# Masking attention weights by comparing exponentials with one constant instead of scores with a threshold per tile

## The chip, the cores and the metric

The kernel runs on one core of one Trainium2 chip. The metric is the device time of one execution in microseconds (us), lower is better. The engines of the core are named as in the profile: PE is the matrix engine (PEld its weight loads), DVE the vector engine, ACT the scalar engine, POOL the GpSimd engine, SP the engine that issues the DMAs. SBUF is the on-chip working memory; PSUM is the small memory that PE writes, in banks.

## What is computed

There are 8 batches of 8 heads, 576 positions, head size 64, then a feed-forward layer on 4608 tokens (512 to 2048 to 512). All inputs and outputs are float32.

```python
scores = scale * np.matmul(q, k.transpose(0, 1, 3, 2))
thresh = np.max(scores, axis=-1, keepdims=True) - tau        # tau = 0.02
scores = np.where(scores >= thresh, scores, -1000000000.0)
scores = scores - np.max(scores, axis=-1, keepdims=True)
attn = np.exp(scores)
attn = attn / (np.sum(attn, axis=-1, keepdims=True) + 1e-09)
attn_out = np.matmul(attn, v)
...
h = x @ w_in                       # x: attn_out, heads side by side
g = np.maximum(h, 0.0) + np.log1p(np.exp(-np.abs(h)))
out = g @ w_out
```

A score survives if it lies within tau of its row's maximum; the others get weight zero.

## The kernel before

The attention is cut into 32 units, a unit being two heads of one batch, and a unit into 9 tiles of 128 query rows by 576 keys, 288 tiles in all. In a unit a row of a tile holds one head's query, tile 4 the rests of both heads. The feed-forward work is cut into chunks of tokens and is dealt out between the attention tiles, a quota of matmuls for each tile, so that PE has work while a tile goes through the other engines.

A tile goes through these steps, and the names are those of the functions:

- `scores` (L490): PE makes the 128 by 576 scores, in two halves of 288 columns, in one of two PSUM buffers `s` (`SB` = 2). The weights and queries are split in high and low parts, so four matmuls (eight in tile 4) make one tile.
- `row_max`: DVE reduces the scores to minus the row's maximum, `negm`.
- `exps`: ACT writes exp(score + negm) into one of the three slots of `e_all` in SBUF (`EB` = 3), and with a second, tiny instruction the threshold `thr` = max - tau.
- `mask`: DVE compares the scores, still in PSUM, with `thr`, multiplies the exponentials by the result, in place, and sums the row.
- For the first five units (`whole`), PE turns the masked tile over by transposes and works in float32. For the others, `weights_hi` has POOL write the float16 high part `h` (scaled by 2 to the 15th) and `weights_lo` has DVE write the low part from `e_all` and `h`; a DMA transposes both (`eT<-h` in the profile), and `values` multiplies them with v (tile `vt`, product `pv`).

Ahead of these, k and q are split (`k`, `q` on POOL, from `kn`, `qn`) and turned over (`tr` on PE, `kT`, `qT` on ACT). In the feed-forward, `hidden` makes `h<-xh,w_i` and `h<-xl,w_i` on PE; ACT applies the softplus into `st`; POOL splits that in two float16 parts `g`; `project` makes `o<-w_o,g`, and ACT or DVE adds it into `acc`. POOL also splits the attention's result (`xp`, then `xh` and `xl`). In the first third of the time the feed-forward's weights are prepared as well: DVE reassembles them from words (`wa_i`, `wa_o` from `wc_i`, `wc_o`), and ACT and POOL split them (`w_i`, `w_o`).

The order of the work is set in two ways. The letters of a string, `PAT`, say which step comes when within a tile: while tile g is dealt with, `R` takes the maximum of tile g+2, `e` its exponentials, `m` masks tile g+1, `h` makes the high part of g+1, `l` the low part of g, `f` is feed-forward work, `S` the scores of tile g+3. So tile g+3's scores take the PSUM buffer that tile g+1 had. From tile 36 on (`TQ`), the instructions of DVE, ACT and POOL keep the order in which they are written, by the class `Queue`; its one line, L156, is the line that the profile shows for nearly all instructions of these three engines. Those of PE and of SP, and all of them before tile 36, are put in order by the compiler's scheduler, which lets an instruction go ahead of others when it thinks its data and buffers free.

Of the kernel before, what the change touches and what calls it, by code (L numbers as in the profile page):

```python
# [9 lines left out]
F32 = mybir.dt.float32  # L10
# [3 lines left out]
AF = mybir.ActivationFunctionType  # L14
ALU = mybir.AluOpType
AX = mybir.AxisListType
# [8 lines left out]
P = 128  # L25
# [40 lines left out]
def tile_kernel(ctx: ExitStack, tc: tile.TileContext, q, k, v, tau, w_in, w_out, out):  # L66
# [8 lines left out]
    nc = tc.nc  # L75
# [5 lines left out]
    HS = S // 2  # L81
# [7 lines left out]
    cpool = ctx.enter_context(tc.tile_pool(name="cpool", bufs=1))  # L89
    wpool = ctx.enter_context(tc.tile_pool(name="wpool", bufs=3))  # L90
    apool = ctx.enter_context(tc.tile_pool(name="apool", bufs=2))
# [17 lines left out]
    ntau = cpool.tile([P, 1], F32, name="ntau")  # L109
    nc.vector.tensor_scalar(out=ntau, in0=tau_sb, scalar1=-1.0, scalar2=None, op0=ALU.mult)  # L110
    nc.vector.tensor_tensor(out=ntau, in0=ntau, in1=tau_sb, op=ALU.min)
    qscale = cpool.tile([P, 1], F32, name="qscale")
    nc.vector.tensor_scalar(out=qscale, in0=tau_sb, scalar1=0.0, scalar2=SCALE,
                            op0=ALU.is_ge, op1=ALU.mult)
# [48 lines left out]
    vec = Queue(nc.vector)  # L163
    act = Queue(nc.scalar)
# [172 lines left out]
    for b in range(B):  # L337
        for hp in range(NPAIR):
            s = Unit()
# [151 lines left out]
                                 start=(m == 0), stop=(m == len(parts) - 1))  # L491

    def row_max(s, t):
        negm = apool.tile([P, 1], F32, tag="negm", bufs=3, name=f"negm_{s.i}_{t}")
        thr = apool.tile([P, 1], F32, tag="thr", bufs=3, name=f"thr_{s.i}_{t}")
        vec.reduce_max(negm, s.sp[t][:, :, 0:HS], axis=AX.XY, negate=True)
        s.m[t] = (negm, thr)

    def exps(s, t):
        act.activation(s.e[t].rearrange("p (h n) -> p h n", h=2), s.sp[t][:, :, 0:HS],  # L500
                             AF.Exp, bias=s.m[t][0], scale=1.0)
        act.activation(s.m[t][1], s.m[t][0], AF.Identity, bias=ntau, scale=-1.0)

    def mask(s, t):
        e2 = s.e[t].rearrange("p (h n) -> p h n", h=2)
        masked.append(vec.scalar_tensor_tensor(
            out=e2, in0=s.sp.pop(t)[:, :, 0:HS], scalar=s.m.pop(t)[1], in1=e2, op0=ALU.is_ge, op1=ALU.mult,
            accum_out=s.sums[:, t:t + 1]))

# [419 lines left out]
    for kind, g in WL:  # L931
        for m in range(4):
            n = len(prep)
# [74 lines left out]
    u0.eng, u0.eng_lo = eng, pool  # L1008
    scores(*tiles[0])
    row_max(*tiles[0])  # L1010
    exps(*tiles[0])
    scores(*tiles[1])
    row_max(*tiles[1])
    exps(*tiles[1])
    mask(*tiles[0])
    scores(*tiles[2])
    load_v(units[1])

    done = 0.0
    for g, (cur, t) in enumerate(tiles):  # L1020
# [7 lines left out]
        for step in PAT:  # L1028
# [6 lines left out]
            elif step == "h" and nxt and not nxt[0].whole:  # L1035
                weights_hi(*nxt)
            elif step == "l" and not cur.whole:
                weights_lo(cur, t)
            elif step == "R" and ahead:
                row_max(*ahead)  # L1040
            elif step == "e" and ahead:
                exps(*ahead)
            elif step == "m" and nxt:
                mask(*nxt)
            elif step == "f":
                upto += quota / PAT.count("f")
                while done < upto:
                    done += next(ffn)
            elif step == "x":
                extras(cur.i, t)  # L1050
            elif step == "S" and g + 3 < NS:
                scores(*tiles[g + 3])
            elif step == "v":
                slow_products()
            elif step == "w":
                while prep and prep[0][0] <= g:
                    _, f, a = prep.pop(0)
                    f(*a)
            elif step == "p":
                point()  # L1060
# [40 lines left out]
```

## Time and profile before

| | |
|---|---|
| median of 3 runs | 1302.42 us (1301.31 to 1306.54) |
| the profiled execution | 1300.2 us, of it the span of instructions 1298.4 us |
| PE busy | 1231.9 us, 95% of the span |
| DVE, ACT, POOL busy | 931.2, 906.2, 912.7 us |

The span has four stretches: about 20 us of start; up to about 400 us attention together with the preparation of the weights (the whole units up to 167 us); up to 1147 us attention together with feed-forward chunks; and then feed-forward work alone. Busy times are sums over the span; what an engine's time is worth in one stretch is read from the views of that stretch. "Idle before" in a group, and the list of waits, say which instruction ended an engine's idle time. A matmul's shown time overlaps with the next one's, so a busy PE can still hold short gaps.

### The profile page before, as it was taken

The numbers are of one execution on the slowest core, as the hardware profiler recorded it, in microseconds if no ns is written. First come the engines' busy times: TensorE is split into PE (matmuls) and PEld (weight loads), VectorE is DVE, ScalarE is ACT, GpSimd is POOL, SyncE is SP. The second block draws the span as 40 slices with busy tenths as digits, with TensorE's granted clock in tenths as the row PEclk, the third lists the DMA queues.
The fourth block names the chain that finished last, engine by engine and source line by source line (L and its number), as shares of the span: only waits on it lengthen the run. The fifth ranks groups of instructions, "written<-read, shape, count | busy, mean of one in ns | idle before, by whom it ended". The sixth has DMA issues, their size and how long they took to land.

```text
span 1298.4 us, 21573 instructions
## 1 busy us (share of the span) xinstructions
PE 1231.9 (95%) x7045; PEld 741.9 (57%) x7045; DVE 931.2 (72%) x1738; ACT 906.2 (70%) x1715; POOL 912.7 (70%) x986
## 2 busy tenths in 40 slices
PE   6988987898999999999999999999999999999998
PEld 5655544454566566556555655665657755554455
DVE  6878888989878887788778977786677666640111
ACT  5877887877777777777777787778676767744321
POOL 2577788978876787778776886688667777564332
PEclk9999999999999999999999999999999999999999
DMA  4544458865877788778777787787667665520010
GB/s 130 161 140 125 129 131 166 174 123 122 174 146 147 144 168 163 151 144 175 144 148 144 168 148 148 145 153 147 129 128 162 115 132 106 101 66 17 1 42 17
DMA packets 368737, 167.90 MB, mean 129 GB/s; under 512 B 320208, under 2 KB 346224, under 8 KB 368624
## 3 DMA queue, kind: packets, MB, share of 16 engines
q1 hardware_dynamic: 368624, 166.52, 61.6%
q8 instruction: 56, 0.92, 0.3%
q14 instruction: 57, 0.47, 0.1%
HBM read 56.62 MB, written 10.63 MB: 52 GB/s over the span
## 4 chain that ended last, share of the span: by engine, by line
PE 42%; ACT 17%; DVE 15%; POOL 13%; issue 8%; DMA 4%; SPq 0%; POOLq 0%; DVEq 0%; ACTq 0%
PE o L789 14%; PE h L725 14%; PE s L490 7%; ACT st L156 5%; ACT L156 5%; POOL g L156 4%; DVE e_all L156 3%; DVE h L156 3%; PE pv L605 3%; DVE negm L156 3%; ACT e_all L156 2%; PE pv L559 2%; POOL xl L156 2%; DMA eT<-h 2%; POOL h L156 2%
## 5 line engine op out<-in xcount | busy, mean ns | idle before, releaser
L789 PE MATMUL o<-w_o,g 128*128 128x512 f16 x1728 | 407.1, 381 | 3.3 <-DVE xp L156 1.5
L725 PE MATMUL h<-xh,w_i 128*128 128x512 f16 (+1 forms) x1280 | 361.3, 359 | 4.5 <-ACT kT L156 2.0
L156 POOL TENSOR_SCALAR h<-e_all 128x576 f16<-128x576 f32 x243 | 228.5, 943 | 112.6 <-DVE e_all L156 110.3
L156 ACT ACTIVATE e_all<-s,negm 128x576 f32<-128x576 f32 x288 | 213.6, 742 | 116.6 <-DVE negm L156 110.5
L725 PEld LDWEIGHTS <-w_i 128*128 128x128 f16 x1920 | 179.9, 98 | 168.8 <-issue 11.7
L156 DVE SCALAR_TENSOR_TENSOR e_all<-s,thr,e_all 128x576 f32<-128x576 f32 x288 | 232.8, 809 | 48.9 <-ACT thr L156 48.8
L156 DVE TENSOR_REDUCE negm<-s 128x1 f32<-128x576 f32 x288 | 214.9, 746 | 66.5 <-PE s L490 64.8
L789 PEld LDWEIGHTS <-g 128*128 128x128 f16 x1728 | 159.7, 98 | 176.4 <-issue 7.0
L156 DVE SCALAR_TENSOR_TENSOR h<-e_all,h 128x576 f16<-128x576 f32 x243 | 236.4, 973 | 20.2 <-POOL h L156 19.6
L725 PE MATMUL h<-xl,w_i 128*128 128x512 f16 (+1 forms) x640 | 230.2, 360 | 1.4 <-POOL xl L156 1.3
L156 POOL TENSOR_SCALAR g<-st 128x512 f16<-128x512 f32 x144 | 97.8, 679 | 164.6 <-ACT st L156 162.4
L156 DVE SCALAR_TENSOR_TENSOR acc<-o,c,acc 128x512 f32<-128x512 f32 x108 | 80.1, 743 | 154.5 <-PE o L789 154.1
L156 POOL TENSOR_TENSOR g<-st,g 128x512 f16<-128x512 f32 x144 | 171.9, 1194 | 12.0
L490 PE MATMUL s<-kT,q 128*128 128x288 f32 x768 | 152.7, 328 | 19.3 <-DVE e_all L156 16.7
L156 ACT ACT_TABLE_LOAD x119 | 152.7, 1283 | 4.1 <-DVE negm L156 1.9
L490 PEld LDWEIGHTS s<-kT,q 128*128 128x128 f32 x768 | 114.7, 192 | 57.1 <-DVE e_all L156 44.7
L605 PE MATMUL pv<-eT,vt 128*128 128x288 f16 x972 | 140.6, 288 | 3.9 <-DVE xp L156 2.4
L156 ACT ACTIVATE st<-h,c 128x512 f32<-128x512 f32 x144 | 91.0, 683 | 76.3 <-PE h L725 75.5
L490 PE MATMUL s<-kT,qT 128*128 128x288 f32 x512 | 106.2, 329 | 10.1 <-DVE e_all L156 9.8
L605 PEld LDWEIGHTS <-vt 128*128 128x128 f16 x972 | 89.3, 98 | 38.1 <-issue 5.3
L156 ACT COPY xp<-pv 64x288 f32<-64x288 f32 (+3 forms) x133 | 50.5, 384 | 78.3 <-PE pv L605 74.1
L156 ACT ACTIVATE st<-st,c 128x512 f32<-128x512 f32 x144 | 96.2, 715 | 2.3
(112 smaller groups left out, 1513.8 us busy)
## 6 DMA issues: line engine op xcount, KB each, us to landing
q<-q SPq DMA_DIRECT2D x62, 192.0 KB
kn<-in_k_dram SPq DMA_DIRECT2D x32, 256.0 KB
qn<-in_q_dram SPq DMA_DIRECT2D x32, 256.0 KB
vn<-in_v_dram SPq DMA_DIRECT2D x32, 256.0 KB
wc_i<-in_moe_w_in_dram SPq DMA_DIRECT2D x16, 512.0 KB
wc_o<-in_moe_w_out_dram SPq DMA_DIRECT2D x16, 512.0 KB
qT<-qT SPq DMA_DIRECT2D x62, 128.0 KB
out_dram<-acc SPq DMA_DIRECT2D x14, 512.0 KB
```

The source lines that it names most:

```text
L156: i = getattr(self.eng, name)(*args, **kwargs)
L490: nc.tensor.matmul(sp[:, hf, 0:HS], lhs, s.kT[j][:, hf * HS:(hf + 1) * HS], start=(m == 0), stop=(m == len(parts) - 1))
L559: nc.tensor.matmul(o[0:D, 0:n], s.vn[k_, v_slot(j, c), :], h[k_, c, 0:n], start=(c == 0), stop=(c == NC))
L605: nc.tensor.matmul(o[:, 0:HS], s.vt[:, a, :], s.eT[j][:, b, x0:x0 + HS], start=(n == 0), stop=(n == 2 * NC))
L725: nc.tensor.matmul(bank[:, i * u.T:(i + 1) * u.T], wi[g, cc][:, a, e], x[cc], start=(cc == 0 and m == 0), stop=(cc == NCC - 1 and m == 2))
L789: nc.tensor.matmul(o, u.g[fc][m // 2][:, sl], wo[fc][:, m % 2, :], start=(n == 0), stop=(n == 3 * QF - 1))
```

## The change

Once, at the start, ACT makes `cut` = exp(-tau) (`ntau`, an existing column, is -tau). The mask compares a tile's exponentials with `cut`, as exp(s - max) >= exp(-tau) says the same as s >= max - tau. The threshold `thr` of each tile is no longer made. The mask's two tensor inputs are then both the tile's slot of `e_all` in SBUF; before, one was `e_all` and the other the scores in PSUM. The scores are last read by the exponentials.

```diff
+    cut = cpool.tile([P, 1], F32, name="cut")
+    nc.scalar.activation(cut, ntau, AF.Exp)
...
     def row_max(s, t):
-        negm = apool.tile([P, 1], F32, tag="negm", bufs=3, name=f"negm_{s.i}_{t}")
-        thr = apool.tile([P, 1], F32, tag="thr", bufs=3, name=f"thr_{s.i}_{t}")
-        vec.reduce_max(negm, s.sp[t][:, :, 0:HS], axis=AX.XY, negate=True)
-        s.m[t] = (negm, thr)
+        s.m[t] = apool.tile([P, 1], F32, tag="negm", bufs=3, name=f"negm_{s.i}_{t}")
+        vec.reduce_max(s.m[t], s.sp[t][:, :, 0:HS], axis=AX.XY, negate=True)

     def exps(s, t):
-        act.activation(s.e[t].rearrange("p (h n) -> p h n", h=2), s.sp[t][:, :, 0:HS],
-                             AF.Exp, bias=s.m[t][0], scale=1.0)
-        act.activation(s.m[t][1], s.m[t][0], AF.Identity, bias=ntau, scale=-1.0)
+        act.activation(s.e[t].rearrange("p (h n) -> p h n", h=2), s.sp.pop(t)[:, :, 0:HS],
+                       AF.Exp, bias=s.m.pop(t), scale=1.0)

     def mask(s, t):
-        e2 = s.e[t].rearrange("p (h n) -> p h n", h=2)
         masked.append(vec.scalar_tensor_tensor(
-            out=e2, in0=s.sp.pop(t)[:, :, 0:HS], scalar=s.m.pop(t)[1], in1=e2, op0=ALU.is_ge, op1=ALU.mult,
-            accum_out=s.sums[:, t:t + 1]))
+            out=s.e[t], in0=s.e[t], scalar=cut, in1=s.e[t], op0=ALU.is_ge, op1=ALU.mult, accum_out=s.sums[:, t:t + 1]))
```

On DVE the order of a tile's steps stays. Before, around tiles 2 to 4 of a unit in the third stretch (`s` are the score buffers, `h` the float16 weights, numbers at the ends of names only tell tiles apart):

```order
L156 TENSOR_REDUCE negm_3_6721<-s_131 128x1
L156 SCALAR_TENSOR_TENSOR e_all,sums_6576<-s_130,thr_2_6687,e_all 128x576
L156 SCALAR_TENSOR_TENSOR h_132<-e_all,h_132 128x576
L156 TENSOR_REDUCE negm_4_6757<-s_130 128x1
L156 SCALAR_TENSOR_TENSOR e_all,sums_6576<-s_131,thr_3_6722,e_all 128x576
L156 SCALAR_TENSOR_TENSOR h_132<-e_all,h_132 128x576
```

and with the change, at the same place on DVE (L158 is the same line, two lines further down):

```order
L158 TENSOR_REDUCE negm_3_6429<-s_133 128x1
L158 SCALAR_TENSOR_TENSOR e_all,sums_6290<-e_all,cut 128x576
L158 SCALAR_TENSOR_TENSOR h_134<-e_all,h_134 128x576
L158 TENSOR_REDUCE negm_4_6463<-s_132 128x1
L158 SCALAR_TENSOR_TENSOR e_all,sums_6290<-e_all,cut 128x576
L158 SCALAR_TENSOR_TENSOR h_134<-e_all,h_134 128x576
```

Nothing moved there: the maximum, the mask and the low part follow each other as before, and only what the mask reads is another.

On ACT at that place stands before (`st` is the softplus of a feed-forward block):

```order
L156 ACTIVATE e_all<-s_130,negm_2_6686 128x576
L156 ACTIVATE thr_2_6687<-negm_2_6686,ntau 128x1
L156 ACTIVATE e_all<-s_131,negm_3_6721 128x576
L156 ACTIVATE thr_3_6722<-negm_3_6721,ntau 128x1
L156 ACTIVATE rt_6754<-rT_6746 9x128
L156 ACTIVATE e_all<-s_130,negm_4_6757 128x576
L156 ACTIVATE thr_4_6758<-negm_4_6757,ntau 128x1
L156 ACT_TABLE_LOAD
L156 ACTIVATE st_15_6788<-h_15_6734,c_2_5147 128x512
```

and now:

```order
L158 ACTIVATE e_all<-s_132,negm_2_6396 128x576
L158 ACTIVATE e_all<-s_133,negm_3_6429 128x576
L158 ACTIVATE rt_6460<-rT_6452 9x128
L158 ACTIVATE e_all<-s_132,negm_4_6463 128x576
L158 ACT_TABLE_LOAD
L158 ACTIVATE st_15_6492<-h_15_6440,c_2_4923 128x512
```

One instruction a tile is gone, and the rest keeps its order.

On PE the scheduler puts some tiles' scores earlier among the other matmuls, as it thinks their buffer free sooner. This is most marked in the second stretch. Before, the scores of tile 1 of unit 7 stand inside the output block `o_1_2`, whose first products are already behind them:

```order
L789 LDWEIGHTS g_0_5_2362
L789 MATMUL o_1_2_2904<-w_o_1_2104,g_0_5_2362 128x512
L490 MATMUL s_130<-kT_0_2657,q_95 128x288 x4
L789 LDWEIGHTS g_0_5_2363
L789 MATMUL o_1_2_2904<-w_o_1_2104,g_0_5_2363 128x512
L789 LDWEIGHTS g_0_6_2697
```

and now the same scores stand ahead of that block:

```order
L787 LDWEIGHTS g_0_7_2616
L787 MATMUL o_1_1_2725<-w_o_3_2109,g_0_7_2616 128x512
L432 MATMUL tr_1_1_2741<-identr,q_7_1_2649 128x128 x4
L492 MATMUL s_132<-kT_0_2541,q_97 128x288 x4
L787 LDWEIGHTS g_0_4_2236
L787 MATMUL o_1_2_2778<-w_o_0_1961,g_0_4_2236 128x512
```

So these scores moved ahead of some products of the feed-forward and of the values; elsewhere in the third stretch most scores stand where they stood.

## The prediction

> **What bounds the kernel now.** I read the totals first, then the busy times by stretch, then the waits of PE, and last the single instructions around a mask.
>
> ```profile
> span 1298.4 us, 21573 instructions
> PE 1231.9 (95%) x7045; PEld 741.9 (57%) x7045; DVE 931.2 (72%) x1738; ACT 906.2 (70%) x1715; POOL 912.7 (70%) x986
> ...
> 20.00:400.00 380.00, 342.89 (x1886) 207.78 (x1885) 323.54 (x609) 304.66 (x641) 291.38 (x301) 0.98 0.61 140
> 400.00:1147.00 747.00, 736.10 (x4351) 451.75 (x4349) 575.48 (x1070) 547.49 (x984) 557.33 (x604) 1.00 0.73 143
> ...
> 240.00:280.00 40.00, 33.09 (x183) 19.68 (x182) 39.49 (x70) 29.79 (x60) 31.16 (x29) 0.96 0.69 144
> 320.00:360.00 40.00, 39.08 (x230) 24.13 (x231) 34.34 (x61) 29.50 (x53) 33.38 (x36) 1.00 0.81 173
> ```
>
> A row by stretch gives its length, then the busy us of PE, PEld, DVE, ACT and POOL, the granted clock, and the share and rate of the DMAs. From 400 to 1147 us PE is busy 736 of 747 us: PE sets the time, and the other engines have a quarter to spare (DVE 171.5 us idle, POOL 189.7). From 20 to 400 us PE has 37 us of gaps, and DVE is the tightest of the others with 56.5 us idle. The last two rows show how far DVE may be loaded: at 34.3 of 40 us PE still runs at 39.1; at 39.5 of 40 PE is down to 33.1. What is left outside these stretches, start and end, has two masks or none.
>
> ```profile
> PE s L490 <- DVE e_all L156: 26.5, 31, 3.3
> PE s L490 <- DVE e_all L156: 18.5, 18, 1.9
> PE s L490 <- DVE e_all L156: 4.8, 12, 0.6
> ```
>
> These are the waits of PE's scores for the mask to give the PSUM buffer back: over the whole span, from 20 to 400 us, and from 400 to 1147 us (us in total, times, longest).
>
> **The change part by part.**
>
> *The buffer comes free sooner.* It is now given back by the exponentials, and these run a step of the tile pipeline ahead of the mask. That takes away at most the 26.5 us above. But scores that come early are worth PE time only where the rest keeps up, and some scores now stand earlier on PE, ahead of products that could have run meanwhile. I take half of the first part (-9 us of 18.5, at 20 to 400 us) and most of the second (-4 us of 4.8); ends 0 and -26.5.
>
> *The threshold goes from ACT, and DVE's wait for it.*
>
> ```profile
> L156 ACT ACTIVATE thr<-negm,ntau 128x1 f32<-128x1 f32 x288 | 83.2, 289 | 0.1
> L156 DVE SCALAR_TENSOR_TENSOR e_all<-s,thr,e_all 128x576 f32<-128x576 f32 x97 | 78.4, 809 | 14.6 <-ACT thr L156 14.6
> L156 DVE SCALAR_TENSOR_TENSOR e_all<-s,thr,e_all 128x576 f32<-128x576 f32 x189 | 152.8, 809 | 34.2 <-ACT thr L156 34.2
> ```
>
> ACT loses 83.2 us of 906. ACT bounds no stretch (304.66 of 380, 547.49 of 747), so by itself this is worth nothing. The two mask rows are those of 20 to 400 and 400 to 1147 us (97 and 189 masks): DVE waited 48 times for `thr`; the exponentials come 0.29 us earlier than `thr` did, so 48 x 0.29 = 14 us of DVE's idle time goes, which is idle time and not work. I count it as cover for what follows, not as a gain.
>
> *The mask reads SBUF twice.* This is the term that decides.
>
> ```profile
> L156 DVE SCALAR_TENSOR_TENSOR e_all<-s,thr,e_all x288: 798/808/819, 17.4 to 1144.3; 128x576 f32<-128x576 f32 x144
> L156 POOL TENSOR_SCALAR h<-e_all x243: 661/1112/1717, 167.2 to 1145.2; 128x576 f16<-128x576 f32 x122
> L156 DVE SCALAR_TENSOR_TENSOR h<-e_all,h x243: 744/916/1999, 171.0 to 1146.8; 128x576 f16<-128x576 f32 x122
> L156 DVE TENSOR_TENSOR xp<-pv,xp x108: 439/456/463, 216.0 to 1158.8; 64x288 f32<-64x288 f32 x108
> L156 DVE SCALAR_TENSOR_TENSOR wa_o<-wc_o,wa_o x32: 673/1096/1815, 81.3 to 278.9; 128x512 uint32<-128x512 uint32 x32
> ...
> 605.78 0.75 DVE L156 SCALAR_TENSOR_TENSOR h<-e_all,h 128x576 f16<-128x576 f32 x1
> 605.95 1.11 POOL L156 TENSOR_SCALAR h<-e_all 128x576 f16<-128x576 f32 x1 [1.07 <-DVE e_all L156]
> 607.49 0.80 DVE L156 SCALAR_TENSOR_TENSOR e_all<-s,thr,e_all 128x576 f32<-128x576 f32 x1
> 607.78 1.41 POOL L156 TENSOR_TENSOR k<-kn,k 128x576 fp32r<-128x576 f32 x1
> 608.22 1.58 DVE L156 SCALAR_TENSOR_TENSOR h<-e_all,h 128x576 f16<-128x576 f32 x1
> ```
>
> The first five rows give the shortest, the middle and the longest duration in ns. Instructions of DVE with one input in PSUM (the mask, `xp<-pv,xp`) always take the same time. Those with both inputs in SBUF (`h<-e_all,h`, `wa_o<-wc_o,wa_o`) take up to 2.7 times their shortest. The five rows of the timeline (start, duration) show why: POOL's `k` ran from 607.78 to 609.19; DVE's low part, begun at 608.22, ended at 609.80, 0.61 us after POOL's end. The other way round, DVE's low part ended at 606.53, and POOL's `h`, begun at 605.95, at 607.06, 0.53 us after it. Such a pair doesn't overlap in its main part. The mask at 607.49, with one SBUF input, ran its 0.80 us while POOL's `k` began and took no longer. With the change the mask belongs to the other kind.
>
> In "SBUF — State Buffer", section "Who interferes with whom", the Trainium skill states the same split: a DVE instruction with two SBUF inputs contends with a GpSimd instruction that reads SBUF, one with at most one such input does not. This speaks against the change, and the rows here bear it out.
>
> Alone, the new mask should take the 744 ns of the low part of the same 576 columns, 0.065 us under today's 809. Its wait for POOL isn't in the trace. From below: the low part's own mean wait, 973 - 744 = 229 ns, from the row at the end of this part. From above: POOL is in an instruction for 291.38 / 380 = 0.77 of 20 to 400 us, a mean one lasts 291.38 / 301 = 0.97 us, and if each mask had to wait for a whole one that is 0.74 us. I take half a POOL instruction, as a mask can come at any point of it: 0.77 x 0.48 = 0.37 us; and 557.33 / 747 x 0.46 = 0.34 us for 400 to 1147 us. Net of the 0.065 us, that is 97 x 0.305 = 30 us more DVE time in the second stretch and 189 x 0.275 = 52 us in the third. No cover is left if DVE's idle time ends.
>
> Behind the mask on DVE stands the low part. A POOL instruction that the mask held up goes first when the mask ends, and then holds up the low part: I take 0.1 us for each of the 243 (5 us and 19 us by stretch), between 0 and 0.4. POOL in turn is held up by masks, at most 0.61 us each; of its 88.6 us idle at 20 to 400 us and 189.7 us later the masks take 97 x 0.77 x 0.61 = 46 us and 189 x 0.75 x 0.61 = 86 us at most. POOL stays under its stretch's length.
>
> What is late next, then, is DVE. At 20 to 400 us it gets 35 us more work, 323.5 + 35 = 358.5 of 380, between the two 40 us rows above. Half of the 35, 17.5 us, I let through to the end, as some of DVE's idle time is true waiting for ACT, POOL and PE. From 400 to 1147 us it becomes 575.5 + 71 = 646 of 747 = 0.87, as loaded as at 320 to 360 us, where PE kept 0.98: I let 8% through, 6 us.
>
> ```profile
> L156 DVE SCALAR_TENSOR_TENSOR h<-e_all,h 128x576 f16<-128x576 f32 x243 | 236.4, 973 | 20.2 <-POOL h L156 19.6
> ...
> 3.66 0.16 DVE L111 TENSOR_TENSOR ntau<-ntau,tau_sb 128x1 f32<-128x1 f32 x1
> 5.04 0.67 ACT L156 CAST k<-kn 128x576 fp32r<-128x576 f32 x1 [3.02 <-DMA kn<-in_k_dram]
> ```
>
> *The constant.* It is ACT's first instruction, ready when `ntau` is, at 3.82 us, and short as `thr`, 0.29 us: done at 4.1, while ACT waits for `kn` until 5.04. It costs nothing, and if `kn` came a microsecond earlier, a few tenths.
>
> **The sum.** -9 - 4 + 17.5 + 6 = +10.5 us on the profiled execution's 1300.2 us. The median of the runs, 1302.4, lies 2.2 us above that execution, so the forecast is 1300.2 + 10.5 + 2.2, about 1313 us.
>
> **The rivals.**
>
> *The early buffer wins (the other side).* If the mask's two inputs, which are one and the same tile, go by one read, it doesn't hold POOL up; no row shows an instruction that reads one tile twice. Or POOL and DVE have the slack to take the waits. Then the 26.5 us of waits for the buffer go, less a fifth for scores that now wait for the exponentials: -21 us, 1281 us. It decides where the mask's mean wait stays under some 0.1 us, or where less than a fifth of DVE's added work comes through. For it speaks that the scores' start hung on the mask in 31 waits of PE; against it, the split of the rows above, without an exception.
>
> *Hidden anyway.* DVE's idle time of 56.5 and 171.5 us takes the new waits, and the saving at the buffer is as large as what comes through: 1302 us. For it speaks the row of 320 to 360 us; against it 240 to 280 us, where DVE has half a microsecond left.
>
> *The port is the bound.* The same section of the Trainium skill says that the lock is exclusive and is held for the full instruction. As a mechanism of this kernel: if a pair of such instructions could not overlap at all, POOL's 848.7 us from 20 to 1147, less the 243 x (943 - 661 ns) = 68 us that its `h` already waits, and DVE's 243 x 0.744 + 64 x 0.673 (`wa_i` taken as `wa_o`) + 288 x 0.744 us would have to fit one after another: 781 + 438 = 1219 us in 1127, 92 us too much.
>
> ```profile
> L156 POOL TENSOR_SCALAR h<-e_all 128x576 f16<-128x576 f32 x243 | 228.5, 943 | 112.6 <-DVE e_all L156 110.3
> ```
>
> The trace bears it out in part: what follows the release is 0.61 of 0.744 us and 0.53 of 0.661 us, so each instruction overlaps by 0.13 us, and over 905 of POOL's and 595 of DVE's that gives 195 us back. It then fits, at 0.91 of the time. As other POOL rows also hold waits, 92 us is an upper end; I set this rival at +60 us, 1362.
>
> **How the numbers follow.** Some of the new waits come through (1306 to 1345, likeliest 1313): 0.43. Hidden (1296 to 1309): 0.24, of which a fifth lies on either side. The early buffer wins (1272 to 1296): 0.25. The port as the bound (1345 to 1380): 0.08. A change of under 0.5%, 6.5 us, can't be told from none here. So faster 0.27, same 0.26, slower 0.47. The slower case's own range is 1306 to 1345; the range that leaves 2 in 10 out reaches from 1279, into the early buffer's case, to 1346.
>
> **What would show it.** The mask's shortest time near 744 ns, its middle near 1.0 us and its longest near 2 us would show the contention; 740 to 760 throughout would show the one read. POOL's `k`, `g` and `q`, whose shortest times are whole today, should lengthen on average. No `thr` on ACT, and the scores' waits named after ACT's `e_all` and much shorter. DVE near 358 of 380 us in the second stretch if the sum holds. I am wrong if PE's gaps from 20 to 400 us shrink below 30 us (the early buffer wins), or if PE from 400 to 1147 us falls under 0.96 (the port).

## The result, and the profile after

The kernel with the change takes 1356.2 us (median of 4 runs, 1355.58 to 1356.88), the kernel before 1301.87 us in the runs beside it: 1.041 times as long, with an interval of 1.038 to 1.044. The direction of the forecast was right; its size was not: +54 us against +10.5, and outside the range.

The totals of the profile after:

```profile
span 1353.8 us, 21257 instructions
PE 1241.1 (92%) x7045; PEld 756.4 (56%) x7045; DVE 1033.2 (76%) x1738; ACT 855.0 (63%) x1428; POOL 999.8 (74%) x986
...
PEclk9988889889999999999999999999999999999999
```

DVE's busy time grew by 102.0 us and POOL's by 87.1, with the same number of instructions on each; ACT lost 51 us. Neither DVE nor POOL is near the span.

The two stretches of attention (length, then PE, DVE, ACT and POOL as in the prediction's rows; the third stretch ends with the last mask, which now lies near 1200 us):

```profile
20.00:400.00 380.00, 325.62 (x1742) 200.36 (x1742) 339.55 (x578) 269.26 (x515) 301.02 (x281) 0.93 0.56 131
400.00:1200.00 800.00, 758.82 (x4475) 471.35 (x4474) 657.68 (x1095) 532.13 (x824) 632.44 (x623) 0.99 0.70 137
```

From 20 to 400 us PE did 1742 matmuls instead of 1886, and at the rate of before 144 of them are 29 us. From 400 to 1200 us it did 4475, which at the rate of before (4351 in 747 us) would have taken 768 us: 32 us. The counts are rough (together 61 us, where the span grew by 55), but by them the loss comes about half from each stretch, though only a third of the masks lie in the first. The two lose in different ways. Up to 400 us, PE's idle time grew from 37 to 54 us, and the mean matmul got longer (325.62 / 1742 = 0.187 us of busy time, 0.182 before); the granted clock fell from 0.98 to 0.93. After 400 us nearly all of the loss is idle time, which grew from 11 to 41 us.

The mask, the low part and POOL's `h` (shortest, middle and longest in ns), then the groups with the mean and what ended the idle time before them:

```profile
L158 DVE SCALAR_TENSOR_TENSOR e_all<-e_all,cut x288: 799/825/2019, 18.1 to 1201.7; 128x576 f32<-128x576 f32 x144
L158 DVE SCALAR_TENSOR_TENSOR h<-e_all,h x243: 743/995/1972, 184.4 to 1203.8; 128x576 f16<-128x576 f32 x122
L158 POOL TENSOR_SCALAR h<-e_all x243: 660/1112/1197, 180.6 to 1202.6; 128x576 f16<-128x576 f32 x122
...
L158 DVE SCALAR_TENSOR_TENSOR e_all<-e_all,cut 128x576 f32<-128x576 f32 x288 | 295.7, 1027 | 26.4 <-ACT e_all L158 26.2
L158 DVE SCALAR_TENSOR_TENSOR h<-e_all,h 128x576 f16<-128x576 f32 x243 | 273.6, 1126 | 42.2 <-POOL h L158 42.2
L158 POOL TENSOR_TENSOR vt<-vn,vt 128x640 f16<-128x640 f32 x27 | 48.2, 1786 | 2.3
```

and POOL's `vt` before:

```profile
L156 POOL TENSOR_TENSOR vt<-vn,vt 128x640 f16<-128x640 f32 x27 | 39.4, 1459 | 2.3
```

The mask, which never left 798 to 819 ns before, now takes up to 2019: it contends. Its mean grew from 809 to 1027 ns (288 x 0.218 = 63 us), the low part's from 973 to 1126 (243 x 0.153 = 37 us). POOL's `vt` took 1459 ns before and takes 1786.

Five of PE's waits after (us, times, longest; `s` is the one for the score buffer, `topv` a small tile made from v), and the instruction of PE that gained most idle time ahead of it, after (L425) and before (L423):

```profile
PE tr L425 <- DVE xp L158: 32.6, 16, 2.5
...
PE tr L425 <- DVE topv L158: 6.0, 1, 6.0
...
PE pv L603 <- DVE xp L158: 4.9, 5, 1.1
...
PE s L492 <- ACT e_all L158: 4.1, 3, 2.2
...
PE o L787 <- DVE xp L158: 3.7, 3, 1.8
...
L425 PE MATMUL tr<-identr,k 128*128 128x128 f32 x64 | 20.2, 316 | 43.5 <-DVE xp L158 32.6 <-DVE topv L158 6.0 <-ACT gw L158 2.6
```

```profile
L423 PE MATMUL tr<-identr,k 128*128 128x128 f32 x64 | 20.4, 318 | 2.0 <-DVE acc L156 0.7 <-DVE xp L156 0.5 <-ACT gw L156 0.2
```

The wait for the score buffer went from 26.5 to 4.1 us, as the early release promised. In its place PE now idles 43.5 us, 2.0 before, ahead of the transposes of k, mostly until DVE's `xp<-pv,xp` gives a PSUM buffer back. Of the 32.6 us of that wait only 3.6 lie before 400 us, so it is a matter of the time after that. How it comes about is seen at the end of a unit, in the timeline of after (start, duration):

```profile
600.83 1.21 DVE L158 SCALAR_TENSOR_TENSOR h<-e_all,h 128x576 f16<-128x576 f32 x1 [1.68 <-POOL h L158]
...
602.63 0.80 DVE L158 SCALAR_TENSOR_TENSOR e_all<-e_all,cut 128x576 f32<-128x576 f32 x1
602.71 1.98 POOL L158 TENSOR_TENSOR vt<-vn,vt 128x640 f16<-128x640 f32 x1
...
603.36 1.93 DVE L158 SCALAR_TENSOR_TENSOR h<-e_all,h 128x576 f16<-128x576 f32 x1
...
605.22 0.44 DVE L158 TENSOR_TENSOR xp<-pv,xp 64x288 f32<-64x288 f32 x1
...
605.72 0.28 PE L425 MATMUL tr<-identr,k 128*128 128x128 f32 x1 [2.53 <-DVE xp L158]
```

The mask, begun at 602.63, holds up POOL's `vt`; that then has its turn and holds up DVE's low part until 605.29, 1.93 us instead of the 0.74 that it takes alone. `xp` stands behind the low part on DVE, and PE's transpose behind `xp`. So 1.93 less 0.74, about 1.2 us, of the 2.53 us for which PE idles here go back to this collision, with a mask that itself waited for nothing. DVE was late already, as the low part before had waited 1.68 us for POOL's `h`.

### The profile page after: what moved, and what is told of

Its sections match the earlier page's. It is cut to its first block, busy times and chain, and to the rows that moved or that the text cites. A ratio compares the mean times of both kernels' runs of the same rounds, so it can differ in the third digit from the quotient of the medians.

```text
span 1353.8 us, 21257 instructions
## 1 busy us (share of the span) xinstructions
PE 1241.1 (92%) x7045; PEld 756.4 (56%) x7045; DVE 1033.2 (76%) x1738; ACT 855.0 (63%) x1428; POOL 999.8 (74%) x986
## 4 chain that ended last, share of the span: by engine, by line
PE 29%; POOL 22%; DVE 22%; issue 12%; ACT 9%; DMA 4%; SPq 1%; POOLq 0%; ACTq 0%; DVEq 0%
PE o L787 11%; PE h L723 10%; POOL g L158 7%; DVE e_all L158 5%; DVE h L158 5%; DVE negm L158 5%; POOL h L158 4%; PE s L492 3%; ACT st L158 3%; ACT L158 2%; PE pv L603 2%; POOL xl L158 2%; DVE wa_o L158 2%; POOL q L158 2%; ACT e_all L158 2%
## 5 line engine op out<-in xcount | busy, mean ns | idle before, releaser
L787 PE MATMUL o<-w_o,g 128*128 128x512 f16 x1728 | 412.9, 387 | 5.5 <-DVE xp L158 3.7
L723 PE MATMUL h<-xh,w_i 128*128 128x512 f16 (+1 forms) x1280 | 366.1, 363 | 8.7 <-ACT kT L158 4.9
L158 ACT ACTIVATE e_all<-s,negm 128x576 f32<-128x576 f32 x288 | 212.5, 742 | 194.7 <-DVE negm L158 184.0
L158 POOL TENSOR_SCALAR h<-e_all 128x576 f16<-128x576 f32 x243 | 229.9, 949 | 118.5 <-DVE e_all L158 118.2
L158 DVE SCALAR_TENSOR_TENSOR e_all<-e_all,cut 128x576 f32<-128x576 f32 x288 | 295.7, 1027 | 26.4 <-ACT e_all L158 26.2
L158 DVE SCALAR_TENSOR_TENSOR h<-e_all,h 128x576 f16<-128x576 f32 x243 | 273.6, 1126 | 42.2 <-POOL h L158 42.2
L787 PEld LDWEIGHTS <-g 128*128 128x128 f16 x1728 | 163.1, 99 | 185.5 <-issue 18.1
L158 DVE TENSOR_REDUCE negm<-s 128x1 f32<-128x576 f32 x288 | 214.6, 745 | 45.5 <-PE s L492 44.3
L158 POOL TENSOR_SCALAR g<-st 128x512 f16<-128x512 f32 x144 | 109.2, 758 | 137.8 <-ACT st L158 129.4
L158 POOL TENSOR_TENSOR g<-st,g 128x512 f16<-128x512 f32 x144 | 185.2, 1286 | 12.0
L158 DVE SCALAR_TENSOR_TENSOR acc<-o,c,acc 128x512 f32<-128x512 f32 x108 | 80.1, 743 | 136.0 <-PE o L787 135.2
L492 PE MATMUL s<-kT,q 128*128 128x288 f32 x768 | 160.4, 338 | 7.0 <-ACT e_all L158 4.1
L158 ACT ACTIVATE st<-h,c 128x512 f32<-128x512 f32 x144 | 91.1, 684 | 78.9 <-PE h L723 78.2
L492 PEld LDWEIGHTS s<-kT,q 128*128 128x128 f32 x768 | 121.7, 198 | 29.4 <-ACT e_all L158 7.0
L158 ACT ACTIVATE st<-st,c 128x512 f32<-128x512 f32 x144 | 96.2, 715 | 2.3
L492 PEld LDWEIGHTS s<-kT,qT 128*128 128x128 f32 x512 | 79.4, 190 | 12.9 <-ACT e_all L158 0.8
```

The source lines that it names most:

```text
L158: i = getattr(self.eng, name)(*args, **kwargs)
L492: nc.tensor.matmul(sp[:, hf, 0:HS], lhs, s.kT[j][:, hf * HS:(hf + 1) * HS], start=(m == 0), stop=(m == len(parts) - 1))
L723: nc.tensor.matmul(bank[:, i * u.T:(i + 1) * u.T], wi[g, cc][:, a, e], x[cc], start=(cc == 0 and m == 0), stop=(cc == NCC - 1 and m == 2))
L787: nc.tensor.matmul(o, u.g[fc][m // 2][:, sl], wo[fc][:, m % 2, :], start=(n == 0), stop=(n == 3 * QF - 1))
```

## The experiments

Times are medians; a ratio is to the kernel before in the same session, with its interval. The median of the kernel before was 1301.87 to 1305.36 us by session, so a difference between runs of two sessions is good to about 3 us.

**The change taken apart.** The first keeps the early release but gives the mask one tensor input. It leaves the masking itself out (a maximum with `cut` in its place), and so do the kernels below that use this mask:

```diff
-        masked.append(vec.scalar_tensor_tensor(
-            out=s.e[t], in0=s.e[t], scalar=cut, in1=s.e[t], op0=ALU.is_ge, op1=ALU.mult, ...
+        masked.append(vec.tensor_scalar(
+            out=s.e[t], in0=s.e[t], scalar1=cut, scalar2=0.0, op0=ALU.max, op1=ALU.add, ...
```

> The changed kernel, but the mask is one DVE instruction over the same 576 columns with a single SBUF tensor input (the larger of the exponential and cut, with the row sum); it leaves out the masking itself. Order on PE and early release of the score buffer stay as in the changed kernel. If the collisions of the mask with POOL are the loss (theory port): back to the kernel before or under it, 1270 to 1300 us, mask durations all within 50 ns of each other, and PE's waits on the xp addition under 8 us. If the loss comes from the scores that stand earlier on PE and the early release (rival order): 1335 to 1356 us.

Measured: 1294.25 us, 0.992 (0.990 to 0.995).

```profile
PE 1222.8 (95%) x7045; PEld 750.2 (58%) x7045; DVE 931.9 (72%) x1738; ACT 855.8 (66%) x1428; POOL 924.2 (72%) x986
...
L158 DVE TENSOR_SCALAR_CACHE_REDUCE e_all<-e_all,cut x288: 793/803/815, 18.0 to 1138.2; 128x576 f32<-128x576 f32 x144
```

So the 62 us between this and the change go with the mask's second SBUF input. The edit also changes the values that later instructions read, but DVE's `xp`, for one, takes 455 ns (its middle) in both kernels. PE's wait for `xp` ahead of the transposes is 10.7 us here, where I had expected under 8. The mask is again as regular as before, but at 803 ns: a pass over SBUF with a row sum isn't shorter than one over PSUM.

The second is the change with the old release: the scores wait for the mask of the tile that had their buffer.

```diff
...
+                if m == 0 and hf == 0 and k_ >= 0:      # k_: the mask of two tiles earlier
+                    tc.add_manual_dep(i.ins, masked[k_].ins.name, ...)
```

> The changed kernel with one wait added: a tile's scores wait for the mask of the tile that used the same score buffer, as before the change. The mask still reads SBUF twice. Theory port: the early release was a gain that is given back here, 1358 to 1385 us. Rival order: the loss goes with the early release, 1300 to 1330 us.

Measured: 1367.96 us, 1.049 (1.047 to 1.050); PE's waits for the buffer:

```profile
PE s L493 <- DVE e_all L158: 71.2, 70, 3.5
```

So the early release is worth about 12 us in the change, where the mask comes late and these waits have grown to 71.2 us.

The third is the kernel before, without `thr` and with `ntau` as the mask's column:

```diff
-        act.activation(s.m[t][1], s.m[t][0], AF.Identity, bias=ntau, scale=-1.0)
...
-            out=e2, in0=s.sp.pop(t)[:, :, 0:HS], scalar=s.m.pop(t)[1], in1=e2, ...
+            out=e2, in0=s.sp.pop(t)[:, :, 0:HS], scalar=ntau, in1=e2, ...
```

> The kernel before without the threshold instruction on ACT: the mask still reads the scores in PSUM, but compares them with the constant column -tau (so the threshold itself is left out of the computation). This does one part of the change alone. If ACT and its threshold bound nothing: 1296 to 1304 us. If the wait of the mask for the threshold was on the path: 1285 to 1295 us, most of the 11 us that the one-input mask gained on the kernel before.

Measured: 1293.92 us, 0.993 (0.991 to 0.995). The threshold, which I had costed at nothing, is worth 8 us. And as the first experiment, which has the early release too, gives the same 1294 us, that release brings nothing where the mask doesn't contend. The change is then, step by step: 1301.9, less 8 without `thr` (1293.9), plus 74 with the mask on SBUF (1368.0), less 12 by the early release (1356.2).

**The same load without collisions.** To the one-input mask come small passes of DVE (72 columns after the mask, one column after the low part), then a small copy of POOL's per tile (104 columns, behind the mask), then both (the copy with 100 columns):

```diff
+        vec.reduce_max(extra[:, 0:1], s.e[t][:, 0:72], axis=AX.X)       # in mask
+        vec.reduce_max(extra[:, 1:2], ntau, axis=AX.X)                  # in weights_lo
```

> The changed kernel with the mask of one SBUF input (masking left out), and two small reductions on DVE that nothing reads: 72 columns behind each mask, one column behind each low part, sized to add about 0.22 and 0.15 us, the mean that a collision added there. DVE gets some 100 us as in the changed kernel, POOL none. If late DVE work alone is the way (theory DVE): 1335 to 1358 us. If it takes both engines holding each other up: 1298 to 1320 us.

```diff
+        pool.tensor_scalar(out=extra, in0=ident[:, 0:104], scalar1=1.0, scalar2=1.0, op0=ALU.mult, op1=ALU.mult)   # in mask
```

> The changed kernel with the mask of one SBUF input (masking left out), and one small POOL copy of 104 columns a tile that nothing reads, about 0.27 us each, 77 us in all, near the 87 us that POOL gained in the changed kernel. If late POOL work alone is the way: 1320 to 1350 us. If POOL's slack of 360 us takes it: 1292 to 1305 us.

> The changed kernel with the mask of one SBUF input (masking left out) and both idle loads together: the two small reductions on DVE (about 0.22 us behind each mask, 0.15 us behind each low part) and the small POOL copy (100 columns, about 0.37 us). Alone they cost 19 and 15 us on the 1294 us of the one-input kernel. If the time of the changed kernel is what two later engines cost together: 1345 to 1360 us. If the loads just add: 1324 to 1334 us, and some 25 us are left that a steady load doesn't show, so that they come from the waits' unevenness.

Measured: 1313.44 us with DVE's load, 1.008 (1.006 to 1.010); 1309.66 with POOL's, 1.005 (1.003 to 1.007); 1328.4 with both, 1.020 (1.019 to 1.022). The totals in this order:

```profile
PE 1227.7 (94%) x7045; PEld 751.9 (57%) x7045; DVE 1025.6 (78%) x2269; ACT 855.8 (65%) x1428; POOL 915.6 (70%) x986
```

```profile
PE 1223.5 (93%) x7045; PEld 749.9 (57%) x7045; DVE 937.8 (72%) x1738; ACT 855.3 (65%) x1428; POOL 999.2 (76%) x1274
```

```profile
PE 1228.7 (93%) x7045; PEld 751.4 (57%) x7045; DVE 1031.1 (78%) x2269; ACT 856.1 (65%) x1428; POOL 996.0 (75%) x1274
```

Over the 1294.25 us of the one-input mask, 94 us more on DVE cost 19 us, 75 more on POOL 15, and both 34: about a fifth each, and they add up. With both, DVE and POOL are as busy as in the change (1033.2, 999.8), and the kernel is 28 us faster than it. So 34 of the 62 us go with the amount of work. The other 28 come with the collisions in some other way. POOL's load alone came out between the two cases named for it: it is neither free nor as dear as I had allowed.

The next puts nearly the same work into bunches, at every third tile (DVE's part behind the low part, at the tiles with t % 3 == 1, isn't printed):

```diff
+        if t % 3 == 2:
+            vec.reduce_max(extra[:, 0:1], s.e[t][:, 0:508], axis=AX.X)
+            for _ in range(3):
+                pool.tensor_scalar(out=extra_p, in0=ident[:, 0:100], ...)
...
```

> As the run with both idle loads (mask of one SBUF input, masking left out), with the same amount of load, but bunched on every third tile: about 0.68 us on DVE behind the mask of tiles 2, 5 and 8 of a unit and 0.43 us behind the low part of tiles 1, 4 and 7, three small POOL copies in a row on tiles 2, 5 and 8. If it is the unevenness of the waits that costs the 28 us which the even loads don't show: 1342 to 1360 us, with over 60 us at half clock. If not: 1324 to 1334 us.

Measured: 1316.57 us, 1.011 (1.010 to 1.013), 12 us less than with even loads (DVE is at 1014.0 here, and 17 us of it are worth 3.5 by the rate above). Both ranges that I had named lie higher. That added work comes in bunches doesn't by itself make it dear.

**Where the collisions lie.** In the change, the masks of two of a unit's nine tiles get the one input: those at the unit's two ends (8 and 0), then two inner ones (2 and 3).

```diff
+        if t in (0, 8):          # in the other kernel: (2, 3)
+            masked.append(vec.tensor_scalar(
+                out=s.e[t], in0=s.e[t], scalar1=cut, scalar2=0.0, op0=ALU.max, op1=ALU.add, ...))
+            return
```

> The changed kernel, but the masks of tiles 8 and 0 of each unit have one SBUF input (the masking of these two in nine is left out). They stand around the end of a unit, where PE waited 43 us for the bank of the xp addition. If each mask's collisions cost alike: 2/9 of the 62 us between the changed and the one-input kernel, so 1340 to 1346 us. If the place of the collision is what counts: 1315 to 1335 us, and those waits of PE under 15 us.

> The same for the masks of tiles 2 and 3, in the middle of a unit. If each mask's collisions cost alike: 1340 to 1346 us, as with tiles 8 and 0. If the place counts: 1346 to 1356 us, and the xp waits of PE stay near 40 us.

Measured: 1330.43 us, 1.021 (1.020 to 1.023), and 1350.56, 1.037 (1.036 to 1.039). The totals, then POOL's `vt` and the wait of PE's transposes for `xp`, of the kernel with 8 and 0 free:

```profile
PE 1228.1 (92%) x7045; PEld 750.3 (56%) x7045; DVE 1006.4 (76%) x1738; ACT 856.1 (64%) x1428; POOL 975.3 (73%) x986
...
L158 POOL TENSOR_TENSOR vt<-vn,vt 128x640 f16<-128x640 f32 x27 | 39.7, 1472 | 2.2
...
PE tr L425 <- DVE xp L158: 28.4, 21, 3.2
```

and of the one with 2 and 3 free:

```profile
PE 1236.2 (92%) x7045; PEld 754.2 (56%) x7045; DVE 1014.4 (75%) x1738; ACT 855.5 (63%) x1428; POOL 987.1 (73%) x986
...
L158 POOL TENSOR_TENSOR vt<-vn,vt 128x640 f16<-128x640 f32 x27 | 48.6, 1800 | 2.3
```

Freeing 2 and 3 takes 19 us off DVE and 13 off POOL, and at a fifth each that is 6 us: measured 6. Freeing 8 and 0 takes off 27 and 25 us, which would be 10: measured 26. The collisions at the unit's ends are dearer than their work, and `vt`, which is split there, is back at its time of before (1459). But PE's wait for `xp` only fell from 32.6 to 28.4 us, where I had expected under 15. So that wait is not the main way by which the ends cost. Of the 24.4 us by which the span got shorter, 13.0 are PE's busy time for the same 7045 matmuls (1241.1 to 1228.1), and 11.4 its idle time.

The next moves the late transpose of k from tile 8 to tile 6, in the change, and in the kernel before:

```diff
-ST = (0, 2, 3, 3, 4, 5, 6, 8)
+ST = (0, 2, 3, 3, 4, 5, 6, 6)
```

> The changed kernel; the transpose of the rest of k for the second head (step 8 of the list ST) is put at tile 6 of a unit and no longer at tile 8, so that it doesn't need the PSUM bank that the xp addition frees. PE's 43 us of idle time ahead of this transpose should go. If that bank is the way by which late DVE work reaches PE: 1315 to 1332 us. If DVE and POOL as a whole set the pace, the wait comes back at other matmuls: 1345 to 1358 us.

> The kernel before with the transpose of the rest of k for the second head at tile 6 of a unit and no longer at tile 8, as in the run of the changed kernel with that move. If the 11 us gained there belong to the late xp addition of the changed kernel: here within 4 us of the kernel before, 1298 to 1306 us. If the place is simply better: 1290 to 1296 us.

Measured: 1345.43 us in the change, 11 less than the change itself; 1309.96 in the kernel before, 8 more, outside both ranges named for it. The totals of the first, its `o` products (mean in ns) and its waits for `xp`, then the `o` products in the change:

```profile
PE 1230.4 (92%) x7045; PEld 753.6 (56%) x7045; DVE 1042.9 (78%) x1738; ACT 853.2 (64%) x1428; POOL 1002.9 (75%) x986
...
L787 PE MATMUL o<-w_o,g 128*128 128x512 f16 x1728 | 405.8, 381 | 12.3 <-DVE xp L158 9.1
...
PE pv L603 <- DVE xp L158: 10.2, 9, 2.0
PE o L787 <- DVE xp L158: 9.1, 11, 1.4
...
PE tr L425 <- DVE xp L158: 4.7, 2, 3.0
```

```profile
L787 PE MATMUL o<-w_o,g 128*128 128x512 f16 x1728 | 412.9, 387 | 5.5 <-DVE xp L158 3.7
```

The transposes lose their wait (32.6 to 4.7), and others get it (`pv` 4.9 to 10.2, `o` 3.7 to 9.1, and more for what ACT gives). PE idles as long as in the change, 1342.9 - 1230.4 = 112.5 us against 1353.8 - 1241.1 = 112.7: the wait has moved, in shorter pieces, and isn't gone. That is the second case of the expectation (1345 to 1358 us, at its lower edge), in which DVE and POOL as a whole set the pace. The 11 us are gained in PE's busy time instead, for the same matmuls: the mean `o` product takes 381 ns and not 387, and the granted clock is 0.983 and not 0.971.

The last of this group writes the low part ahead of the mask:

```diff
-PAT = "RemhlTfpSxfvwp"
+PAT = "RelmhTfpSxfvwp"
```

> The changed kernel with the DVE order of two steps swapped: the low part of tile g ahead of the mask of tile g+1, so that the low part no longer stands right behind a mask that has held POOL up. If it is the pair mask, low part that makes POOL and DVE take turns with whole instructions: DVE's mean low part falls from 1126 to under 1020 ns and the time to 1320 to 1345 us. If only the number of instructions that can't overlap counts: 1350 to 1365 us.

Measured: 1393.16 us, 1.067 (1.064 to 1.070).

```profile
L158 DVE SCALAR_TENSOR_TENSOR h<-e_all,h 128x576 f16<-128x576 f32 x243 | 241.2, 993 | 90.1 <-POOL h L158 86.4
...
PE tr L425 <- DVE xp L158: 57.0, 23, 3.5
```

The low part collides less (993 ns against 1126), the mask more (1110 against 1027), and together they are some 8 us of DVE's time less. But the low part now waits 86.4 us for POOL's `h`, against 42.2 in the change, and the mask stands behind it. A little less in collisions, and 37 us lost, more than either range had: here a wait in DVE's queue costs more than the collisions that it avoids.

**Ways out.** Here ACT makes the high part for all tiles, then for the odd ones; the third is the kernel before with POOL making `thr`:

```diff
-        pool.tensor_scalar(out=h[:, 0:S], in0=s.e[t], scalar1=2.0 ** 15, scalar2=1.0, op0=ALU.mult, op1=ALU.mult)
+        act.activation(h[:, 0:S], s.e[t], AF.Copy, scale=2.0 ** 15)
```

> The changed kernel with the high parts of the weights (128x576, 243 of them) made on ACT and no longer on POOL. POOL loses 230 us, ACT gains about 180 us (855 to 1035). Theory port: fewer POOL instructions to collide with, the masks' mean falls from 1027 to 900 to 960 ns, and the time to 1300 to 1330 us. If ACT, which then waits in order for each mask, becomes the bound: over 1340 us.

> As the run with the high parts on ACT, but only those of a unit's odd tiles (4 of 9): POOL loses about 100 us, ACT gains about 80. Theory port: in between, 1320 to 1340 us. If ACT's in-order wait for the mask is what costs: above 1345 us.

```diff
-        act.activation(s.m[t][1], s.m[t][0], AF.Identity, bias=ntau, scale=-1.0)
+        pool.tensor_scalar(out=s.m[t][1], in0=s.m[t][0], scalar1=-1.0, scalar2=ntau, op0=ALU.mult, op1=ALU.add)
```

> The kernel before with the threshold made by a 128x1 instruction on POOL and no longer on ACT; the mask reads the scores in PSUM as before. Leaving the threshold out gained 8 us. If POOL makes it in time, that gain is had without leaving anything out: 1292 to 1299 us. If it stands behind POOL instructions of 1.2 us and more and the mask waits for it: 1302 to 1325 us.

Measured: 1344.85 us (1.032), 1341.19 (1.030) and 1322.77 (1.015). Totals, the mask and a wait of the first, and the wait of the third:

```profile
PE 1237.7 (92%) x7045; PEld 750.8 (56%) x7045; DVE 989.4 (74%) x1738; ACT 998.4 (74%) x1671; POOL 745.0 (55%) x743
...
L158 DVE SCALAR_TENSOR_TENSOR e_all<-e_all,cut 128x576 f32<-128x576 f32 x288 | 302.9, 1052 | 74.3 <-ACT e_all L158 73.6
...
DVE e_all L158 <- ACT e_all L158: 73.6, 51, 4.5
```

```profile
DVE e_all L156 <- POOL thr L156: 53.2, 42, 2.9
```

POOL loses a quarter of its work in the first, and only 11 us come back. The mask collides as much as ever (1052 ns on average, where I had expected 900 to 960), and DVE now waits 73.6 us for exponentials that stand behind `h` on ACT (26.2 in the change). With the odd tiles alone it is 15 us, a little less than expected. Making `thr` on POOL costs 20 us over the kernel before: it stands in POOL's queue among long passes, and DVE waits for it.

The last computes everything without `thr` and without a second SBUF input: DVE's first pass writes tau minus the scores and takes their least, `c`, for each row, and this one column is both the bias of the exponentials and the threshold of the mask.

```diff
+        vec.tensor_scalar(out=s.e[t].rearrange("p (h n) -> p h n", h=2), in0=s.sp[t][:, :, 0:HS], scalar1=tau_sb,
+                          scalar2=1e30, op0=ALU.add, op1=ALU.min, accum_out=c)     # scores made negative ahead
...
+            out=e2, in0=s.sp.pop(t)[:, :, 0:HS], scalar=s.m.pop(t), in1=e2, op0=ALU.is_le, op1=ALU.mult, ...
```

> A kernel that computes everything, with the mask reading the scores in PSUM as before and no threshold on ACT: PE makes the scores with the other sign, DVE takes the least of score + tau in one pass (written to the tile's slot of e_all, which the exponentials then overwrite), and that one column serves the exponentials as bias and the mask as threshold. DVE's pass should take about 0.80 + 0.08 us in place of 0.746, 40 us more DVE work; ACT loses 83 us. By the even DVE load (94 us cost 19 us) the first costs 8 us, by the run without the threshold the second gains 8 us: 1296 to 1308 us. If the pass also holds POOL up: over 1320 us.

Measured: 1304.33 us, 1.002 (1.001 to 1.003): no gain.

```profile
L156 DVE TENSOR_SCALAR_CACHE_REDUCE e_all<-s,tau_sb 128x576 f32<-128x576 f32 x288 | 232.6, 808 | 73.6 <-PE s L490 70.4
```

The pass with an output takes 808 ns, where the maximum alone takes 746, and DVE is busy for 951.4 us, 932.7 in the third experiment. At a fifth this is 4 of the 10 us that lie between the two; the rest I did not separate.

## Why the prediction was wrong in size

*The contention* was right, in kind and in amount. The mask's range went from 798 to 819 ns to 799 to 2019, and DVE got 102 us more work, against 30 + 52 + 24 = 106. That the sum came out so near is partly luck, as its terms miss in opposite directions (next paragraph). The Trainium skill's rule ("SBUF — State Buffer", section "Who interferes with whom": two SBUF inputs contend with a GpSimd instruction that reads SBUF) agrees, and holds for one tile given as both inputs too. The rival of one read for both falls.

*The mask alone* was not: 0.744 us was expected from the low part, 0.80 measured. The 0.065 us of saving that I took off each wait didn't exist. The waits came out smaller, so that the mask's added time is 63 us and not 82, and the low part's larger (37 us, not 24).

*The early buffer*, -13 us: PE's wait went from 26.5 to 4.1 as expected, and the experiments put the worth at 12 us in the change and at none where the mask is regular. So the size is luck: the 12 us are gained from a wait of 71.2 us that the collisions make, and not from the 26.5 us that I read in the kernel before.

*The threshold*, costed at nothing: worth 8 us. To count it "as cover for what follows, not as a gain" was wrong; whether the 8 us come from DVE's wait or from ACT's 83 us is not shown.

*What comes through* is the step that failed. "Half of the 35" and "8%" let 23.5 of the 106 us through, 22% on the whole. The one-input mask against the change says 62, and 74 without the early release, which I had counted apart. Of the 62, three parts were measured: DVE's added work by itself lets 20% through (19 of 94 us), which is my share. But POOL's added time, for which I asked only whether POOL "stays under its stretch's length", costs as much again (15 of 75 us). And 28 us more come with the collisions beyond the amount of work; the masks at the ends of the units, 8 and 0, cost 16 us beyond theirs, and 2 and 3 nothing. The split by stretch failed too: I gave the third 2 us net of the whole, and by the count above it lost 32. The sign that I gave for the second, DVE near 358 of 380 us, was a poor one: it came to 339.55, since by 400 us less of the work had been done.

*The port as the bound* gave nearly the time that was measured, and PE fell to 758.82 of 800 us, 0.949, under the 0.96 that I had named as its sign. Its mechanism isn't borne out: with the port as the bound, two freed masks of nine would be worth about the same wherever they lie, and they are worth 26 and 6 us; and taking `h` off POOL (745 us busy instead of 1000) should have given much of the loss back, and gave 11 us, though ACT's queue costs something of its own there.

*What stays open* is by which way the 28 us reach PE. Its record splits them into 12.4 us of busy time for the same 7045 matmuls (1241.1 in the change, 1228.7 with both even loads) and 15.4 us of idle time. A candidate for the first is the clock. The mean granted clock of the change, of the kernel with both even loads, and of the one with the late release:

```profile
core 0: 1353.8 us, clock 0.971
```

```profile
core 0: 1326.0 us, clock 0.987
```

```profile
core 0: 1364.9 us, clock 0.987
```

Against a full clock, 1353.8 x 0.029 = 39 us are missing in the change and 1326.0 x 0.013 = 17 in the other, and the 22 us between them are an upper end for what the clock adds to the 28 in these two runs (14 us by the means of four runs each, 0.974 and 0.984). In the Trainium skill, "TensorE: Matmul & The Clock Gate", section "Part 1: The HAM clock gate (the "warmup" mystery)", a PE that was idle for a window of about 3.4 us has its clock halved, which would make a gap of that length cost more than itself. The trace agrees at most in kind: the longest wait for `xp` in the change is 2.5 us, single waits like the 6.0 us for `topv` are few, and the clock is lowest in the first 400 us, where the transposes' waits for `xp` come to 3.6 us. For the clock speaks the moved transpose: the same idle time in shorter pieces, the clock at 0.983, and 10.7 us less of busy time. Against it speaks the late release, which has the higher clock and takes 12 us more, with 1243.6 us of busy time. No run held the clock apart from the gaps, so its share isn't shown.

## What to carry to other kernels

Before an operand moves from PSUM to SBUF, look at what the other input is and who else reads SBUF: the mask's shortest, middle and longest times agreed, and with both inputs in SBUF they no longer did, at a loss of 102 us of busy time on DVE and 87 on POOL. Price added time on every engine that it reaches, POOL as well as DVE: here a fifth of each engine's added time came through while neither was over 80% busy, and the two added up. Then ask where the collisions lie: freeing the masks at the units' ends (two in nine) brought back 26 of 62 us, and freeing two inner ones 6. And before a wait is called the cause, look at the bounding engine's idle time as a whole: one that goes from the list may have moved to the next instructions.

## What the runs showed of the hardware

The row sum seems to have a price: over 576 float32 columns DVE takes 743 ns without one (the low part's shortest) and 793 to 799 with one (the mask's shortest, in the three ways in which its inputs lay). A collision is passed on: in the timeline above the mask at its shortest, 0.80 us, held POOL's `vt` (1.98 us, its mean before was 1.46), and that the low part (1.93 us), so a mask that shows no wait can still be the one that costs. And the contention reaches instructions that were not changed: POOL's `vt` took 22% longer, and went back to 1472 ns when the masks at two tiles of nine had one input.
